# A span's state in one 128x256 tile and 64x64 products, and a new order for the last quarter of w_out and six loads

## The chip, the cores and the metric

The kernel runs on one core of a Trainium2 chip. The time is the device time of one execution in microseconds; the figure compared is the median of several executions. A profile of one execution shows each engine's instructions. The engines are TensorE (PE; its weight loads PEld), VectorE (DVE), ScalarE (ACT), GpSimd (POOL) and SyncE (SP, which only issues transfers here). Each works through its own queue in order and waits on semaphores. Matrix products leave their results in PSUM[...]; VectorE and ScalarE carry them from there to SBUF.

## The reference

Blocked linear attention with a decay per head, and a gated two-layer network on its result. There are 4 batches, 8 heads, 768 positions and 64 numbers per head; blocks of 64 positions; the network goes from 512 to 2048 and back, over 3072 tokens.

```python
for b in range(nb):
    intra = np.einsum('bhic,bhjc->bhij', qb, kb) * Dmask[None]
    intra = np.einsum('bhij,bhjd->bhid', intra, vb)
    inter = np.einsum('bhid,bhde->bhie', qb * lam_pow[None], kv_state)
    out[:, :, sl] = intra + inter
    kv_state = lam_block * kv_state + np.einsum('bhsd,bhse->bhde', kb_dec, vb)
x = out.transpose(0, 2, 1, 3).reshape(B * S, H * D)
h = x @ w_in
return (h * np.cos(h)) @ w_out
```

## The kernel before

**Tiling.** Tokens are worked in 24 sets of 128 ("blocks" in the code). The first four belong to two *spans*: span x is the first 256 positions of batch x, two positions to a partition. The rest form *ordinary pairs* 2 to 11 of two sets each, the same 128 positions of two batches. The network takes its tokens in nine tiles (`TILES`), the first of 512, most of 256. For each tile there are 16 hidden tiles f0 to f15 (L732: four products each, then a cosine on ScalarE, L738, and a product on VectorE, L744), and for each 128 tokens j four groups of four output products (L778), one group for each quarter of w_out. The first tile's hidden tiles f0 to f4 are made in two halves of 256 tokens, span 0's (columns 0 to 255) and span 1's.

**Stages.** At the start q and k of the spans are loaded (SP), scaled (L593; span 1's k on GpSimd), transposed on TensorE (L601) and copied (L604). Scores (L612), masks (L617) and values (L638) follow in two halves, *hp* 0 and 1, of four heads. The state that the second 128 positions of a span take from its first 128 is made by L625 from rows 0 to 63 (two heads at a time, 64x128 products of which only the diagonal 64x64 blocks are wanted), cast block by block into the block-diagonal `kv_bd` (L629, two instructions), and read by four full 128x128 products (L644), which add to the values in PSUM. `kv_bd` is filled with zeros beforehand (L217). Casts L652 then write `xT`, the input of the hidden products. Later, L697 makes the state at the end of both spans for pair 2.

An ordinary pair has six loads, q_f, k_f and v_f twice; scaled or cast copies (L329, L333, L337); transposes (pair 2 on TensorE, L359, later ones by DMA from SP's queue, L365); scores L407, mask L412, values L470 (L487 is a one-element copy that makes two row halves take turns), state products L419, sums L425, casts L430, carried products L502.

**What sets the order.** A planner at build time. Each piece of work is a task with an engine, an assumed length, what it depends on and a priority; the planner sets them on a time line, and each engine's queue has the order of that line. So changed assumed lengths move instructions. Between TensorE's tasks, until a certain hidden tile, `keep_awake` puts filler products into gaps of the plan (L866, 128x512 in bf16; L870 in f32). Loads of the spans, of w_in and w_out and of the pairs are issued in the order of the string `ORDER`: q, k, v with a number are loads from SP (spans' v from GpSimd), i0 to i5 pieces of w_in and o0 to o3 quarters of w_out, from GpSimd. In it o3 waited for the landing of the first load of pair 2 (q4, its first q_f), and v4 for k4; q4 itself waits, before and after, for tile 0's f13 (`pace`).

## Time and profile before

| | us |
|---|---|
| median of three executions | 202.84 (202.67 to 203.12) |
| the profiled execution | 202.54 |
| its span, first to last instruction | 200.80 |
| mean granted TensorE clock | 0.998 |

```profile
PE   6999999999999999999999999999999999999994
DVE  3978771269756948758458575835588354444001
ACT  4878771149658768666639666644887564345120
POOL 5893003085235360635555353545500000000000
DMA  5999999999889997999999899979910010111112
```

Each digit is the busy share of a fortieth of the span (5.02 us) in tenths; 9 is 90% or more. TensorE is at 9 from the second slice to the last but one. The DMA engines are at 9 or near it until seven tenths of the span, when the loads are done.

In the chain of waits, a row is the start, the length, and the engine with the tile, the line and the number of instructions; rows follow each other in time. In the time line of one engine, the second column is the time from the first start to the last modelled end, so neighbouring rows can overlap; the difference between two starts is what the first group really took from the engine. "DMA to landing" tells the least, the median and the most time from a transfer's issue to its end.

### The profile page before, as it was taken

To read this page: it belongs to the slowest core of one execution; us is meant where nothing else is said; L and a number is where in the kernel's file an instruction comes from. 1 tells how busy PE (TensorE), PEld (TensorE's weight loads), DVE (VectorE), ACT (ScalarE), POOL (GpSimd) and SP (SyncE) were. 2 spreads that over 40 slices of the span, in tenths; PEclk is the share of its full clock that TensorE was granted. 3 is DMA by queue.
4 is the path that set the end of the run, shared out by engine and by line. 5 is a ranking of instruction groups with operands and counts; after the bars stand their busy time and mean duration, and the time that the engine had idled before them with its cause. 6 is when DMAs were issued, how large, how long until landed. Compare 5 with 4: busy or idle time off the path is not lost.

```text
span 200.8 us, 5951 instructions
## 1 busy us (share of the span) xinstructions
PE 195.9 (98%) x2473; PEld 116.8 (58%) x2473; DVE 116.3 (58%) x230; ACT 119.4 (59%) x241; POOL 64.9 (32%) x85
## 2 busy tenths in 40 slices
PE   6999999999999999999999999999999999999994
PEld 3477444558757757766658676755445544444452
DVE  3978771269756948758458575835588354444001
ACT  4878771149658768666639666644887564345120
POOL 5893003085235360635555353545500000000000
PEclk9999999999999999999999999999999999999999
DMA  5999999999889997999999899979910010111112
GB/s 163 303 190 204 203 199 216 209 238 225 200 197 225 262 202 177 239 179 253 189 275 245 188 207 194 277 141 261 243 23 3 3 52 0 52 55 52 52 52 104
DMA packets 96620, 33.93 MB, mean 169 GB/s; under 512 B 84690, under 2 KB 93650, under 8 KB 96594
## 3 DMA queue, kind: packets, MB, share of 16 engines
q1 hardware_dynamic: 89088, 28.78, 63.2%
q0 software_dynamic: 7360, 4.72, 16.4%
q8 instruction: 19, 0.31, 0.7%
q10 hardware_dynamic: 146, 0.07, 0.1%
q14 instruction: 7, 0.06, 0.1%
HBM read 27.26 MB, written 6.29 MB: 167 GB/s over the span
## 4 chain that ended last, share of the span: by engine, by line
PE 95%; DMA 2%; ACT 0%; DVE 0%; SPq 0%; issue 0%; ACTq 0%; DVEq 0%
PE ps_h L732 42%; PE ps_f L778 42%; DMA sp_f<-in_k_dram 2%; PE ps_s L407 2%; PE ps_o L502 2%; PE ps_o L470 2%; PE ps_kv L419 1%; PE ps_t L601 1%; PE ps_s L612 1%; PE ps_o L638 1%; PE ps_kv L625 1%; PE ps_x L470 0%; PE ps_idle L870 0%; PE ps_t L359 0%; DVE k_sp L593 0%; PE ps_o L644 0%
## 5 line engine op out<-in xcount | busy, mean ns | idle before, releaser
L744 DVE TENSOR_TENSOR g<-ps_h,cos 128x256 bf16<-128x256 f32 (+1 forms) x149 | 73.1, 501 | 42.0 <-ACT cos L738 41.1
L738 ACT ACTIVATE cos<-ps_h,halfpi 128x256 f32<-128x256 f32 (+1 forms) x149 | 75.9, 536 | 29.3 <-PE ps_h L732 28.2
L778 PE MATMUL ps_f<-w_out_sb,g 128*128 128x512 bf16 (+2 forms) x400 | 91.4, 371 | 0.0
L732 PE MATMUL ps_h<-xT,w_in_sb 128*128 128x256 bf16 (+1 forms) x596 | 91.1, 303 | 0.0
L732 PEld LDWEIGHTS <-w_in_sb 128*128 128x128 bf16 x596 | 57.5, 98 | 30.1 <-DVE xT L510 0.4
L778 PEld LDWEIGHTS <-g 128*128 128x128 bf16 x400 | 37.6, 98 | 37.2
L329 POOL TENSOR_TENSOR qk<-q_f,q_scale 128x512 bf16<-128x512 f32 x19 | 20.0, 1067 | 34.7 <-DMA q_f<-in_q_dram 17.6
L792 ACT COPY o_sb<-ps_f 128x512 f32<-128x512 f32 (+1 forms) x24 | 13.7, 572 | 24.7 <-PE ps_f L778 24.5
L337 POOL TENSOR_TENSOR v_s<-v_f,v_scale 128x512 bf16<-128x512 f32 x19 | 19.6, 1042 | 9.8 <-DMA v_f<-in_v_dram 5.2
L412 DVE TENSOR_TENSOR s_m<-ps_s,mask 128x512 bf16<-128x512 f32 x20 | 13.0, 685 | 4.2 <-PE ps_s L407 3.6
L333 POOL CAST qk<-k_f 128x512 bf16<-128x512 f32 x18 | 11.0, 611 | 10.4 <-DMA k_f<-in_k_dram 10.2
L510 ACT CAST xT<-ps_o 128x512 bf16<-128x512 f32 x11 | 6.0, 588 | 9.0 <-PE ps_o L502 5.6
L425 DVE TENSOR_TENSOR sum<-sum,ps_kv 128x512 f32<-128x512 f32 x15 | 10.2, 682 | 0.6
L430 ACT CAST S<-sum 128x512 bf16<-128x512 f32 x15 | 9.1, 616 | 0.9 <-DVE sum L425 0.8
L253 POOL DMA_DIRECT2D w_out_sb<-in_moe_w_out_dram x4 | 3.0, 784 | 15.8 <-DMA q_f<-in_q_dram 15.8
L792 DVE COPY o_sb<-ps_f 128x384 f32<-128x384 f32 x1 | 0.6, 557 | 11.6 <-DMA out_dram<-o_sb 11.6
L470 PEld LDWEIGHTS <-v_s 64*64 64x64 bf16 x320 | 4.0, 107 | 4.2 <-issue 3.4
L870 PE MATMUL ps_idle<-blank 128*128 128x512 f32 (+2 forms) x8 | 4.7, 707 | 1.7 <-DVE blank L215 1.7
L487 DVE COPY spare<-ps_o 1x1 f32<-1x1 f32 x6 | 0.9, 156 | 8.4 <-PE ps_o L470 8.4
L617 DVE TENSOR_TENSOR s_m_sp<-ps_s,mask_sp 128x512 bf16<-128x512 f32 x8 | 5.1, 684 | 1.2 <-PE ps_s L612 1.2
L470 PE MATMUL ps_o<-s_m,v_s 64*64 64x64 bf16 x256 | 5.2, 196 | 0.0
L502 PE MATMUL ps_o<-qkT,S 64*64 64x64 bf16 x304 | 4.9, 195 | 0.0
(76 smaller groups left out, 90.1 us busy)
## 6 DMA issues: line engine op xcount, KB each, us to landing
q_f<-in_q_dram SPq DMA_DIRECT2D x20, 256.0 KB, 3.9
k_f<-in_k_dram SPq DMA_DIRECT2D x20, 256.0 KB, 4.2
v_f<-in_v_dram SPq DMA_DIRECT2D x20, 256.0 KB, 5.1
out_dram<-o_sb SPq DMA_DIRECT2D x19, 256.0 KB, 2.5
w_out_sb<-in_moe_w_out_dram POOLq DMA_DIRECT2D x4, 512.0 KB, 12.4
sp_f<-in_q_dram SPq DMA_DIRECT2D x2, 512.0 KB, 4.9
sp_f<-in_k_dram SPq DMA_DIRECT2D x2, 512.0 KB, 5.5
w_in_sb<-in_moe_w_in_dram POOLq DMA_DIRECT2D x2, 512.0 KB, 8.9
```

Source lines behind the costliest of these rows:

```text
L329: vec[e].tensor_mul(new_qk()[:, 0, :, s], live.pop(("q_f", 2 * pr + s)), q_scale[:, c, :].unsqueeze(2).to_broadcast([P, H, D]))
L333: (nc.scalar.copy if early else nc.gpsimd.tensor_copy)(new_qk()[:, 1, :, s], live.pop(("k_f", 2 * pr + s)))
L337: vec[e].tensor_mul(live["v_s", 2 * pr + s], live.pop(("v_f", 2 * pr + s)), v_scale[:, c, :].unsqueeze(2).to_broadcast([P, H, D]))
L412: nc.vector.tensor_mul(t, live["s", pr][s], mask.unsqueeze(1).to_broadcast([P, H, D]))
L425: nc.vector.tensor_add(new, live["sum", pr, 0] if half else live["sum", pr - 1, 1], live["kv", pr][half])
L430: nc.scalar.copy(new_S(pr, half), live["sum", pr, half])
L470: yield lambda h=h: nc.tensor.matmul(o[halves[h % 2], h // 2], lhsT=live["v_s", n0 + s][m, h, :], rhs=live["s_m", n0 + s][m, h, :], start= ...
L732: nc.tensor.matmul(t[:, :n], lhsT=w_in_sb[:, kd, f * P:(f + 1) * P], rhs=live["xT", i][:, kd, at], start=(kd == 0), stop=(kd == KD - 1))
L738: nc.scalar.activation(c[:, :n], live["h", i, f, at.start][:, :n], AF.Sin, bias=halfpi)
L744: return nc.vector.tensor_mul(live["g", i][:, f, at], live.pop(("h", i, f, at.start))[:, :n], live.pop(("c", i, f, at.start))[:, :n])
L778: nc.tensor.matmul(live["f", i, j, piece][:, :width], lhsT=live["g", i][:, f, j * P:(j + 1) * P], rhs=w_out_sb[:, f, part], start=(f == 0) ...
L792: (nc.scalar.copy if eng == "ACT" else nc.vector.tensor_copy)(o[:, :width], live["f", i, j, piece][:, :width])
```

## The change

State of a span: one 128x256 tile `kv_sp`, heads 2p on partitions 0 to 63 and heads 2p+1 on 64 to 127, made by sixteen 64x64 products, cast by one ScalarE instruction, and read by eight 64x64 products behind a drain of TensorE. The zero fill goes.

```diff
-    kv_bd = consts.tile([P, 2, NP, P], BF16)
-    nc.vector.memset(kv_bd, 0.0)
+    kv_sp = consts.tile([P, SPANS, NP, D], BF16)
...
-            L["kv"] = bank(t.bank[0], [P, NP, P], F32, "ps_kv")
+            L["kv"] = bank(t.bank[0], [P, NP, D], F32, "ps_kv")
...
-                    nc.tensor.matmul(L["kv"][:, p, :], lhsT=L["k"][rows, s, 2 * p:2 * p + 2, :], rhs=L["v"][rows, s, 2 * p:2 * p + 2, :],
+                    for i, h in enumerate(halves):
+                        nc.tensor.matmul(L["kv"][h, p, :], lhsT=L["k"][rows, s, 2 * p + i, :], rhs=L["v"][rows, s, 2 * p + i, :],
...
-        def update_out(_, h, e):
-            (nc.scalar.copy if e == "ACT" else nc.vector.tensor_copy)(kv_bd[h, x, :, h], L["kv"][h, :, h])
+        def update_out(_, e):
+            (nc.scalar.copy if e == "ACT" else nc.vector.tensor_copy)(kv_sp[:, x], L["kv"])
...
         def carried(_):
+            nc.tensor.drain()
             for p in range(NP):
-                nc.tensor.matmul(L["o"][1][:, p, :].rearrange("e (s u) -> e s u", s=2),
-                                 lhsT=kv_bd[:, x, p, :], rhs=L["qT"][:, :, p, chunks[1][0]],
-                                 start=False, stop=True, skip_group_check=True)
+                for h in halves:
+                    nc.tensor.matmul(L["o"][1][h, p, :].rearrange("e (s u) -> e s u", s=2),
+                                     lhsT=kv_sp[h, x, p, :], rhs=L["qT"][h, :, p, chunks[1][0]],
+                                     start=False, stop=True, skip_group_check=True)
```

Loads: o3 is issued directly behind o2 and waits for no load; the six loads of pair 2 follow each other on SP, v4 without a wait for k4.

```diff
-ORDER = "q0 k0 q1 k1 v0 v1 i0 i1 i2 i3 i4 i5 o0 o1 o2 q4 q5 k4 k5 o3"
+ORDER = "q0 k0 q1 k1 v0 v1 i0 i1 i2 i3 i4 i5 o0 o1 o2 o3 q4 q5 k4 k5"
...
-        if name == f"v{2 * SPANS}":
-            deps = [load_t["k_f", 2 * SPANS]]
-        if name == "o3":
-            deps = [load_t["q_f", 2 * SPANS]]
```

Planner: other assumed lengths and starts, other priorities for pair 2, the spans' last state made free of pair 2's scores, and one more dependence, of pair 3's scores on the last VectorE product of the second network tile.

```diff
-    SETUP = {"POOL": 3.7, "DVE": 4.4, "ACT": 6.0, "SP": 0.85, "DMA": 1.95}
+    SETUP = {"POOL": 3.7, "DVE": 4.2, "ACT": 6.1, "SP": 0.85, "DMA": 1.95}
...
-        issue_t[name, n], load_t[name, n] = dma("SP", LOAD_US, 0.85, emit, prio, deps, get=name,
-                                                lat=1.9 if name == "v_f" and n < 2 * SPANS + 2 else 1.0)
+        issue_t[name, n], load_t[name, n] = dma("SP", 0.95 if n < 2 * SPANS + 2 else LOAD_US, 0.85, emit, prio, deps, get=name,
+                                                lat=1.0)
...
-                t = pl.add("PE", MM(P, 8), src + ([T[pr, 0]] if i else []), partial(transposes, i=i), pa(-0.05 + 0.05 * i), banks=1)
+                t = pl.add("PE", MM(P, 8), src, partial(transposes, i=i), pa(-0.05 + 0.05 * i) if pr > SPANS else -900.0, banks=1)
...
-        us = {"DVE": 0.69, "POOL": 1.04}
+        us = {"DVE": 0.62, "POOL": 1.02}
...
-            s1 = pl.add("PE", 0.42, outs, partial(scores, hp=hp), pa(0.1 + 0.1 * hp), banks=2)
+            s1 = pl.add("PE", 0.33, outs, partial(scores, hp=hp), pa(0.1 + 0.1 * hp), banks=2)
...
-        u = pl.add("PE", 16 * QUART + SW, span_deps + s_t.deps, update, prio, banks=1)
-        u.then = s_t
-        s_t.deps.append(u)
+        u = pl.add("PE", 16 * QUART + SW, span_deps + [load_t["q_f", 2 * SPANS]], update, -900.0, banks=1)
...
+                if f == KF - 1:
+                    gates[i] = d
...
-    first_scores, first_update = add_scores(SPANS, prio_attn(2 * SPANS, 0.2))
+    first_scores, first_update = add_scores(SPANS, -900.0)
...
+        if i and pr in alone and pr in (3,):
+            alone[pr].deps.append(gates[i])
```

In the program that results, these queues differ from before. TensorE: a filler of 128x512 stands before the first hidden product; two hidden tiles, f0 and f1, not three, stand before span 1's second values; L697 stands alone between output products, two groups ahead of the transposes of pair 2, which stand some 2 us later in the queue than before; the scores of most later pairs stand a few hidden or output groups earlier. VectorE: pair 2's v_s stands before its two masks. ScalarE: the cast of the spans' last state stands before pair 2's two k casts. SP: the DMA transposes of pairs 3 and 4 stand before a store that they followed.

More of the change, by code (lines that the diff above doesn't have):

```diff
@@ L34 @@
 VALUES_OUT = [("ACT", "ACT"), ("DVE", "ACT")]
-STATE_OUT = [("ACT", "ACT"), ("ACT", "ACT")]
-ORDER = "q0 k0 q1 k1 v0 v1 i0 i1 i2 i3 i4 i5 o0 o1 o2 q4 q5 k4 k5 o3"
+STATE_OUT = ["ACT", "ACT"]
+ORDER = "q0 k0 q1 k1 v0 v1 i0 i1 i2 i3 i4 i5 o0 o1 o2 o3 q4 q5 k4 k5"
 W_IN = [2, 2, 1, 3, 4, 4]
@@ L624, in update @@
                 for s in range(2):
-                    nc.tensor.matmul(L["kv"][:, p, :], lhsT=L["k"][rows, s, 2 * p:2 * p + 2, :], rhs=L["v"][rows, s, 2 * p:2 * p + 2, :],
-                                     start=(p == 0 and s == 0), stop=True, skip_group_check=True)
-        def update_out(_, h, e):
-            (nc.scalar.copy if e == "ACT" else nc.vector.tensor_copy)(kv_bd[h, x, :, h], L["kv"][h, :, h])
+                    for i, h in enumerate(halves):
+                        nc.tensor.matmul(L["kv"][h, p, :], lhsT=L["k"][rows, s, 2 * p + i, :], rhs=L["v"][rows, s, 2 * p + i, :],
+                                         start=(p == 0 and s == 0), stop=True, skip_group_check=True)
+        def update_out(_, e):
+            (nc.scalar.copy if e == "ACT" else nc.vector.tensor_copy)(kv_sp[:, x], L["kv"])
         def values(task, hp):
@@ L668, in add_span @@
                 t.bank_frees = [[outs[-1]]]
-            s1 = pl.add("PE", 0.42, outs, partial(scores, hp=hp), pa(0.1 + 0.1 * hp), banks=2)
+            s1 = pl.add("PE", 0.33, outs, partial(scores, hp=hp), pa(0.1 + 0.1 * hp), banks=2)
             if x and hp == 0:
                 s_first = s1
-            so[hp] = [pl.add("DVE", 0.69, [s1], partial(scores_out, hp=hp, i=i), pa(0.1 + 0.1 * hp + 0.05 * i)) for i in range(2)]
+            so[hp] = [pl.add("DVE", 0.61, [s1], partial(scores_out, hp=hp, i=i), pa(0.1 + 0.1 * hp + 0.05 * i)) for i in range(2)]
             s1.bank_frees = [[t] for t in so[hp]]
-        u = pl.add("PE", 0.42, v_t + kt + [spans[0].get("carried")], update, pv(0.1), banks=1)
-        Uo_sp[x] = [pl.add(e, 0.4 if e == "ACT" else 0.42, [u], partial(update_out, h=h, e=e), pv(0.1))
-                    for h, e in zip(halves, STATE_OUT[x])]
+        u = pl.add("PE", 0.28, v_t + kt + [spans[0].get("carried")], update, pv(0.1), banks=1)
+        Uo_sp[x] = [pl.add(STATE_OUT[x], 0.4, [u], partial(update_out, e=STATE_OUT[x]), pv(0.1))]
         u.bank_frees = [Uo_sp[x]]
         span_deps.extend(v_t + kt)
-        v0 = pl.add("PE", 0.35, so[0] + v_t + [spans[0].get("carried")], partial(values, hp=0), pv(0.2), banks=2)
-        v1 = pl.add("PE", 0.35, [v0] + so[1], partial(values, hp=1), pv(0.25))
-        second = pl.add("PE", MM(P, 4) + 0.1, [v1] + Uo_sp[x], carried, pv(0.3))
+        v0 = pl.add("PE", 0.33, so[0] + v_t + [spans[0].get("carried")], partial(values, hp=0), pv(0.2), banks=2)
+        v1 = pl.add("PE", 0.33, [v0] + so[1], partial(values, hp=1), pv(0.25))
+        second = pl.add("PE", 0.25, [v1] + Uo_sp[x], carried, pv(0.3))
         for c, (t, e) in enumerate(zip((v1, second), VALUES_OUT[x])):
@@ L711, in add_span_state @@
         u.bank_frees = [[x]]
-    h_last, o_last = {}, {}
+    h_last, o_last, gates = {}, {}, {}
     hid, closing = [], None
@@ L838 @@
         prepare(pr)
-    first_scores, first_update = add_scores(SPANS, prio_attn(2 * SPANS, 0.2))
+    first_scores, first_update = add_scores(SPANS, -900.0)
     add_span_state(first_scores, prio_attn(2 * SPANS, 0.2))
     pr = SPANS
+    alone = {}
     for i in range(len(TILES)):
@@ L844 @@
             if pr + 1 in ALONE:
-                add_scores(pr + 1, prio_attn(2 * pr + 2, 0.2))
+                alone[pr + 1] = add_scores(pr + 1, prio_attn(2 * pr + 2, 0.2))[0]
             add_stretch(pr, first_update if pr == SPANS else None)
```

## The prediction

> **What bounds the kernel now.** I read the page first: busy shares, then the chain that ended last, then the chain in order of time, then TensorE alone from 10 to 17 us.

> ```profile
> PE 195.9 (98%) x2473; PEld 116.8 (58%) x2473; DVE 116.3 (58%) x230; ACT 119.4 (59%) x241; POOL 64.9 (32%) x85
> PE 95%; DMA 2%; ACT 0%; DVE 0%; SPq 0%; issue 0%; ACTq 0%; DVEq 0%
> ```

> TensorE is busy for 98% of the span and carries 95% of the chain. A busy PE need not be a full one, so the chain in order of time has to show whether anything but matmuls stands in it.

> ```profile
> 10.57 0.40 PE ps_t L601 x4
> ...
> 16.31 12.68 PE ps_h L732 x72
> 28.99 6.04 PE ps_f L778 x28
> ...
> 39.38 0.62 PE ps_kv L697 x32
> 40.00 0.38 PE ps_s L407 x32
> ```

> From 10.57 us to the end each piece starts where the one before it stopped. The large pieces run at one rate: 6.04/28 = 0.216 us for an output product (512 columns); in a later row 6.55/60 = 0.109 us for a hidden product of 256 columns. By these rates the 72 products of the second line (28 of 256 columns, 44 of 512) need 3.06 + 9.49 = 12.55 us, so only 0.13 us of waiting is in them (the load of weights at 16.69 waited for a w_in piece). So from 16 us on nothing can be won by earlier data; only fewer TensorE instructions, fewer changes of shape, or that 0.13 us count, and any new wait costs its full length. What may be won otherwise lies before 16 us:

> ```profile
> 10.90 0.62 PE L625 MATMUL ps_kv<-v_sp,k_sp 64*128 64x128 bf16 x8
> 11.45 0.42 PE L638 MATMUL ps_o<-s_m_sp,v_sp 64*64 64x128 bf16 x16
> 11.69 0.39 PE L612 MATMUL ps_s<-qT_sp,kT_sp 64*64 64x128 bf16 x16
> ...
> 12.70 0.40 PE L644 MATMUL ps_o<-qT_sp,kv_bd 128*128 128x128 bf16 x4
> 13.03 0.62 PE L625 MATMUL ps_kv<-v_sp,k_sp 64*128 64x128 bf16 x8
> ...
> 14.14 1.48 PE L732 MATMUL ps_h<-xT,w_in_sb 128*128 128x256 bf16 x12
> 15.56 0.42 PE L638 MATMUL ps_o<-s_m_sp,v_sp 64*64 64x128 bf16 x16
> 15.91 0.40 PE L644 MATMUL ps_o<-qT_sp,kv_bd 128*128 128x128 bf16 x4
> ```

> The first column is the start; the difference to the next start is what a group costs. Here ScalarE is near:

> ```profile
> 12.93 1.08 ACT L652 CAST xT<-ps_o 128x512 bf16<-128x512 f32 x2
> ```

> The first hidden product (14.14) needs both casts, which end at 14.01.

> [...] the 16 products of L638 cost 0.24 us where the next group is 64*64 too (11.45 to 11.69) and 0.35 where it is not (15.56 to 15.91), both behind a change: 0.10 us for one change. The forecast counts them at that price. [...]

> ```profile
> DMA to landing us min/median/max: 13.3/14.3/15.2
> DMA to landing us min/median/max: 6.6/6.6/6.6
> DMA to landing us min/median/max: 3.3/3.5/3.8
> DMA to landing us min/median/max: 6.2/6.4/6.7
> ```

> In order: quarters 1 and 2 of w_out (issued 15.19 and 15.92, landing 28.5 and 31.1, so 2.6 us apart); quarter 3 (32.55, 39.1); the two q_f of pair 2 (28.74 and 29.15; 32.0 and 32.9); its two v_f (33.89 and 34.31; 40.1 and 41.0). Both times the first load landed 0.9 us behind a quarter under way, and the next 0.9 us later. I go by the trace: loads land behind the quarter, 0.9 us apart.

> **The change part by part.**

> *The zero fill of kv_bd* (0.48 us of VectorE at 1.66) goes; VectorE then idles until 3.93 anyway: nothing.

> *State products.* L625 costs 0.55 us: 0.45 of work and a change. The new form has 16 products 64*64 of 64 columns, of which two run side by side (both use rows 0 to 63). Nearest row: L697, also in twos, (0.62 - 0.10)/32 = 0.016 us each, so 0.26. Span 0 saves 0.19 and the change to L638 behind it, 0.29 in all; span 1 saves 0.19 and both its changes, 0.39. The single cast frees 0.37 us of ScalarE (L629: two take 0.74) at 11.55, where it idles 0.16 us before the next copy anyway: nothing.

> *Carried products.* Eight 64*64 of 128 columns, two by two, cost what four full ones do (12.70 to 13.03 less a change): 0.23. The change before them goes, but a drain stands there. The trace has no drain. From below 0.10[...]; from above 0.6: the tail of a group, 0.18 (it ends 0.42 after its start but costs 0.24), and 0.4, the longest stretch that the list of waits puts down to "issue" before a weight load. I take 0.25, tail and one weight load. Span 0: -0.10 + 0.25, and its change to L625 is counted above. Span 1: the change in front goes, one behind it (to L732) comes: +0.25.

> *What of this is on the path.* Up to the first hidden product the sum is -0.29 - 0.39 - 0.10 + 0.25 = -0.53, but it can't show. k_sp on GpSimd, the transposes, the kT copy (to 11.59), the scores, the second transposes and copy (12.45 to 13.03) and the xT casts keep their times, as each waits for the one before, not for L625. And the order of the changed program has a new filler product (128x512, 0.21 us, with a change) before the first hidden one. So that starts at 14.06 to 14.15 where it was 14.14: I take -0.05.

> *From there to f5* (the first 512-column hidden tile) the set of products is the same; only two hidden tiles instead of three stand before span 1's second values. Those need VectorE's last mask product, which with scores 0.25 us earlier ends near 15.05 and is awaited for some 0.05. Drain: +0.25. The wait for w_in (0.13) vanishes, as f4, whose piece lands at 16.65, now comes after 17.5. Sum -0.05 + 0.05 + 0.25 - 0.13 = +0.12.

> *State of the spans* (L697) moves ahead by itself, between output products; before, it adjoined the scores L407. One more change: +0.10. Counting changes through both orders from 16 us to the end gives 34 and 35, all other products equal in number.

> *w_out's quarter 3 and the six loads.* The quarter is issued by GpSimd at about 16.7, not at 32.55, and needs no wait for q_f any more; nothing but qk of pair 2 stands behind it there. It lands at 31.1 + 2.6 = 33.7. The loads, still held by L744's f13 until 28.74 on SP, then land at 34.6, 35.5 (q), 36.4, 37.3 (k), 38.2, 39.1 (v) instead of 32.0 to 41.0: q later, v earlier. TensorE asks for them in a new order: transposes of q at 37.4 (VectorE and GpSimd ready 36.6), of k at 38.7 (ScalarE first casts the span state until 37.3, then k twice until 38.4), scores at 41.0, values at 43.2. For these VectorE runs v_s ahead of the masks (two, 1.29): 41.5 to 42.85. All covers hold, the smallest by 0.3 us. No wait was there before, so nothing is won: 0. If the cover fails, the excess is paid in full.

> *SP's and the later order.* Transposes of pairs 3 and 4 go ahead of a store, and scores of pairs 4 to 11 move up against the hidden products by up to 2 us. qkT landed 0.7 us or more ahead of the new places even at the old times, and the stores have no reader: 0. The gate on pair 3's scores waits for a VectorE product done 0.7 us earlier: 0.

> **Sum.** +0.12 + 0.10 = +0.22 us. The profiled execution took 202.54 (span 200.80, 1.74 around it), giving 202.76; the median of the runs shown is 202.84, 0.3 above the profiled one. On that base 203.06, rounded to 203.05.

> **Rivals.**
> *Slower, by pair 2's loads.* Before quarter 3 the old run has an empty gap: k's last load landed near 34.7, the quarter at 39.1 took 2.6, so 1.8 us moved nothing, with v's loads already issued. If such a gap now stands between quarters 2 and 3, all six loads slide by it. GpSimd's qk is then ready at 36.6 + 1.8 = 38.4 where TensorE's queue holds the transposes L359 at 37.4, with every output product behind them: 1.0 us, and 204.1 in all. It decides from a gap of 0.8. For: the old gap. Against: the quarter is now queued behind another[...].
> *Faster: TensorE's saving counts in full.* The chain names TensorE before 14 us too. If the casts come earlier with it and a drain costs 0.10: -0.68 up to the first hidden product, then 0.10 - 0.13 + 0.10, in all -0.61; 202.2. Against: the chain of copies and casts, and the filler.
> *Not what it says:* moved scores or a transposed load find their data late somewhere after 46 us (stalls of a few tenths, pair 4 or 6): 203.6. For: places moved by 1 to 2 us; against: the margins above.

> **Chances.** My forecast 0.67, with its own range 202.75 to 203.55 (drain 0.1 to 0.6, and some 0.15 for the median); loads 0.17; faster 0.07; later stalls 0.09. What a measurement here can tell from no change is 0.2%, 0.4 us. Of my forecast 0.53 lies within it and 0.14 above; so faster 0.07, same 0.53, slower 0.40. Range 202.6 to 203.9: it leaves out the faster case and most of the loads' one.

> **What would show it.** Right: first L732 at 14.1; the carried products start about 0.3 us behind the values' last issue, not 0.15; f5 some 0.1 later than its old 18.45; L697 between L778 rows with 0.1 us on both sides; quarter 3 landing near 33.7 and v near 39; output products after 46 us offset by a constant 0.2. Wrong: f5 earlier than 18.3 (path not ScalarE's), idle TensorE before L470 near 43, or an offset that grows later.

## The result, and the profile after

| | before | changed |
|---|---|---|
| median of 4 runs (range), us | 202.86 (202.67 to 203.12) | 204.80 (204.56 to 204.88) |
| ratio, 95% interval | | 1.0088, 1.0064 to 1.0113 |
| profiled execution, its span | 202.54, 200.8 | 204.72, 203.0 |

The change costs 1.94 us; 0.2 was forecast, 203.9 was the upper end. The page of the changed kernel, engines and chain:

```profile
PE 194.8 (96%) x2475; PEld 118.2 (58%) x2502; DVE 115.5 (57%) x229; ACT 118.5 (58%) x239; POOL 64.8 (32%) x85
PE 93%; issue 2%; DVE 2%; ACT 2%; ACTq 0%; DVEq 0%
```

The span is 2.2 us longer. The 194.8 us against 195.9 don't mean less work: 27 products lack in the records (2,475, with 2,502 weight loads, one for each product; before 2,473 and 2,473), and the changed kernel with the old fillers (e9 below), whose records are complete, has 196.5. "issue" went from 0% of the chain to 2%: time in which the engine waited for nothing that the profile shows. The chain in order of time says where (start, length, what):

```profile
13.80 1.08 ACT xT L654 x2
14.93 1.03 PE ps_h L731 x8
15.96 0.29 PE ps_o L638 x12
16.25 0.54 issue
16.79 0.25 PE ps_o L638 x4
17.16 0.41 PE ps_o L646 x8
...
37.57 0.62 PE ps_kv L698 x32
38.20 0.16 issue
...
131.07 0.48 ACT cos L737
131.55 0.52 ACT S L429
132.06 0.60 PE ps_h L731 x4
```

Three things stand out. The first hidden product comes at 14.93, not 14.14. Sixteen products of one line, span 1's values, are torn into 12 and 4: the last of the 12 issued at 16.04, the next at 16.79, with no semaphore between. And at 132 us another engine stands in the chain where only TensorE stood before (eight hidden products in a row from 131.32). The 0.16 of "issue" at 38.20 is none: the weight load of the next product is there at 38.14, the product itself is one of those that lack. Weight loads tell a true gap. Since a profile is one execution, two of each kernel are set side by side (the second ones are e10 and e4 below):

| us | before | before, again | changed | changed, again |
|---|---|---|---|---|
| first hidden product | 14.14 | 14.70 | 14.93 | 14.40 |
| first output product | 28.82 | 29.28 | 30.50 | 30.22 |
| between the two | 14.68 | 14.58 | 15.57 | 15.82 |
| fifth o_sb copy | 57.34 | 57.80 | 59.12 | 58.92 |
| span | 200.8 | 201.3 | 203.0 | 202.9 |

The means of the two differ by 0.24 us at the first hidden product, 1.31 at the first output product, 1.45 at 57 us and 1.9 at the end. So the 1.9 us are 0.24 of front, 1.07 between 14 and 30 us, 0.14 in the stretch with the span state, and 0.45 late, at 132 us. The front is scatter as much as change: the two executions of one kernel differ by 0.5 us there. One part of it is no scatter. From the last transposes of span 1 (12.02 and 12.57 us before, 12.52 and 11.99 in the change) to the first hidden product it is 2.12 and 2.13 us before, and 2.41 both times in the change. ScalarE's row of the change tells why:

```profile
13.80 1.07 ACT L654 CAST xT<-ps_o 128x512 bf16<-128x512 f32 x2 [0.27 <-PE ps_o L646]
```

In the new program the two casts of span 0 have changed places, which the list of changed queues above leaves out: the first one now waits for the last carried product, behind the drain, and the second has no wait of its own. Before, the first began at 12.93, before the last carried product had ended.

The transfers did what was forecast, up to k. The landing rows of quarters 0 and 1, 2 and 3 of w_out (issued at 14.5, 15.2, 15.9 and 16.7), then of the two q_f of pair 2 (30.4 and 30.8):

```profile
DMA to landing us min/median/max: 11.7/12.6/13.5
DMA to landing us min/median/max: 13.5/15.3/17.1
DMA to landing us min/median/max: 4.3/4.5/4.8
```

Quarter 3 landed at 33.8 (33.7 forecast), q at 34.7 and 35.6 (34.6 and 35.5), the first k at 38.1 (36.4), v at 39.7 and 40.6 (38.2 and 39.1); TensorE waited for none of them.

### The profile page after: what moved, and what is told of

Its sections match the earlier page's. It is cut to its first block, busy times and chain, and to the rows that moved or that the text cites. A ratio compares the mean times of both kernels' runs of the same rounds, so it can differ in the third digit from the quotient of the medians.

```text
span 203.0 us, 5981 instructions
## 1 busy us (share of the span) xinstructions
PE 194.8 (96%) x2475; PEld 118.2 (58%) x2502; DVE 115.5 (57%) x229; ACT 118.5 (58%) x239; POOL 64.8 (32%) x85
## 4 chain that ended last, share of the span: by engine, by line
PE 93%; issue 2%; DVE 2%; ACT 2%; ACTq 0%; DVEq 0%
PE ps_h L731 41%; PE ps_f L779 40%; PE ps_idle L870 3%; PE ps_s L406 1%; PE ps_o L501 1%; PE ps_o L469 1%; PE ps_kv L418 1%; PE ps_t L600 1%; DVE sum L424 1%; DVE s_m L411 1%; PE ps_s L611 1%; ACT xT L654 1%; PE ps_x L469 0%; ACT cos L737 0%; PE ps_t L358 0%
## 5 line engine op out<-in xcount | busy, mean ns | idle before, releaser
L737 ACT ACTIVATE cos<-ps_h,halfpi 128x256 f32<-128x256 f32 (+1 forms) x149 | 75.8, 537 | 30.7 <-PE ps_h L731 30.4
L779 PE MATMUL ps_f<-w_out_sb,g 128*128 128x512 bf16 (+2 forms) x377 | 88.4, 370 | 2.2 <-issue 1.4
L336 POOL TENSOR_TENSOR v_s<-v_f,v_scale 128x512 bf16<-128x512 f32 x19 | 19.7, 1044 | 16.8 <-DMA v_f<-in_v_dram 14.5
L870 PE MATMUL ps_idle<-blank 128*128 128x512 f32 (+3 forms) x12 | 5.9, 620 | 1.7 <-DVE blank L215 1.7
L520 DVE TENSOR_TENSOR xT<-ps_o,cross 128x256 bf16<-128x256 f32 x8 | 3.1, 422 | 3.8 <-PE ps_o L501 3.8
## 6 DMA issues: line engine op xcount, KB each, us to landing
w_out_sb<-in_moe_w_out_dram POOLq DMA_DIRECT2D x4, 512.0 KB, 14.4
```

What stands on the lines that cost most here:

```text
L336: vec[e].tensor_mul(live["v_s", 2 * pr + s], live.pop(("v_f", 2 * pr + s)), v_scale[:, c, :].unsqueeze(2).to_broadcast([P, H, D]))
L737: nc.scalar.activation(c[:, :n], live["h", i, f, at.start][:, :n], AF.Sin, bias=halfpi)
L779: nc.tensor.matmul(live["f", i, j, piece][:, :width], lhsT=live["g", i][:, f, j * P:(j + 1) * P], rhs=w_out_sb[:, f, part], start=(f == 0) ...
L870: nc.tensor.matmul(idle_ps[:, :n], lhsT=blank[:, :P], rhs=blank[:, :n], start=True, stop=True)
```

## The experiments

Two theories were set up. **S, instruction supply**: TensorE's instructions arrive in blocks, and the change, with 24 products more (48 instructions, as each has a weight load) and two drains, reaches the end of a block before the next is there. **F, late front**: new filler products, and a TensorE clock that rises late (7.75 us in the profile of the change, 5.4 before), hold up everything ahead of the first hidden product. What led to S is the page's row of the queue that carries instructions:

```profile
q8 instruction: 19, 0.31, 0.6%
```

Its columns are packets, MB and share of the time. That is 16.4 KB a packet (16,384 bytes in the trace), and 19 packets for TensorE's some 5,000 instructions, so about 256 each (of all kernels here, those with up to 5,030 have 19 packets, those with 5,086 and more have 20). In the trace the first one starts at 14.38 us; the view of the transfers from 14.1 to 14.4 us has it:

```profile
q8 instruction: 1, 0.02, 19.8%
```

**e1 and e2: each half of the change alone.**

```
e1: before, with kv_sp, its 64*64 products, one cast, the drain
e2: changed, with kv_bd, its 128x128 products, two casts, the zero fill
```

> The kernel before with the state part alone: one 128x256 tile, 64x64 products, one cast, the drain; order of loads, lengths in the planner and fillers as before. Instruction supply (theory S: TensorE's stream comes in blocks; the instructions after about the 450th are there only from 16.75 us on, and the changed kernel gets to that point 1.7 us sooner because its state products are twice as many): TensorE gets there at about 15.7 us, in the second half of span 1's values, and stands still until 16.75, 1.0 us for nothing that the profile names; with 0.2 for the drains the time is 204.0. Late front (theory F: fillers and the TensorE clock): the fillers are the old ones, so the first hidden product comes at 14.1 as before, nothing stalls at 16 us, and the time is 203.1. Drain alone (as predicted): 203.1.

> The changed kernel with the old state tile and its 128x128 products (and the zero-fill), everything else as in the change. S: the 450th instruction is a hidden product at about 18 us, so there is no stall at 16 us; what is left is the late front, 0.7 to 0.8, and the extra change of shape, 0.1: 203.7. F: the late front makes nearly all of the 2 us, so 204.5. If the first hidden product comes at 14.1 here, the late front belongs to the state part.

e1 took 205.29 us (203.87 to 206.59; ratio 1.0103, 1.0061 to 1.0146), e2 203.29 (1.0014, 1.0004 to 1.0025). The state part alone has the stall, again inside span 1's values (15.98 to 16.68, 0.70 us from the last issue before it to the first after; all stalls below are given so); the rest alone has none. F falls as the main cause: e2's first hidden product came later (15.10) than that of e1 (14.39) or of the change, and e2 is the faster one by 2 us. The rest alone costs 0.4, which leaves 1.2 to 1.5 of the change to the state part. e1's second cost was not foreseen. Rows of SyncE, GpSimd, ScalarE and TensorE in its profile, which is the slowest of its six executions (206.59):

```profile
31.15 2.08 SPq L252 DMA_DIRECT2D k_f<-in_k_dram  x2
33.17 0.74 POOL L252 DMA_DIRECT2D w_out_sb<-in_moe_w_out_dram  x1 [16.46 <-DMA q_f<-in_q_dram]
39.69 0.62 ACT L332 CAST qk<-k_f 128x512 bf16<-128x512 f32 x1 [3.58 <-DMA k_f<-in_k_dram]
40.36 0.62 PE L358 MATMUL ps_t<-ident,qk 128*128 128x128 bf16 x8 [2.06 <-ACT qk L332]
```

With the old order of loads, quarter 3 went out while the second k_f was under way, and this k_f was used at 39.69 instead of 35.61 as before: 2.06 us of idle TensorE. So e1's time says little on the state part by itself. In the new order quarter 3 lands at 33.8, ahead of all six loads; how often the race is lost with the old order is not shown.

**e3, e4: more instructions in the kernel before; the change again.**

```
-  matmul(idle_ps, lhsT=ident, rhs=ident.unsqueeze(1).to_broadcast([P, 4, P]))
+  for j in range(8):
+      matmul(idle_ps[:, 64 * j:64 * j + 64], lhsT=ident, rhs=ident[:, :64])
```

> The kernel before, with each of its three 512-column fillers on ident issued as eight of 64 columns: the same columns, 42 more instructions ahead of the first hidden product, the computation untouched. S: the 450th instruction is now in the second half of span 1's values at 15.7 us, and TensorE stands still there until about 16.75: +1.0, 203.9. F and the drain: no change, 202.9.

> The changed kernel once more, for the scatter of its profile. S: the same stall at the same instruction, 16.1 to 16.8 us. If the stall is an accident of one execution, it is not there, and the time is the same all the same. F: if the late TensorE clock (full only from 7.75 us in the first profile, 5.4 before) belongs to the kernel, it is at 7.75 again; if it is chance, it lies elsewhere, and the first hidden product moves with it while the time stays within 204.6 to 204.9 only if something later sets it.

e4: 204.51 (1.0072, 1.0047 to 1.0097). The stall is at the same instruction, 15.51 to 16.51, 1.00 us where the first execution has 0.76, although the front was 0.5 us earlier: TensorE ran ahead and waited longer. The clock rose at 6.48. So the clock is chance and the stall is not. e3: 203.76 (1.0042, 1.0024 to 1.0061), the expected size by luck, since the place is another. The packet started at 13.41, in time; there was no stall at 16 us. Instead a piece of w_in landed at 15.88 (14.94 before), and TensorE stood 0.56 us waiting for it; and 0.57 us went at 132 us, by "issue", where the kernel before has 0.11 from load to load:

```profile
132.69 0.83 PE L732 MATMUL ps_h<-xT,w_in_sb 128*128 128x256 bf16 x6 [0.29 <-issue]
```

This stall and those of the changed kernel (131.56 to 132.06), e4 and e1 stand at one number in the records of TensorE, the 3,756th or 3,757th. The records lack 21 products by then. Counted by weight loads, which are complete, 3,777 instructions are out in each of the four, and the one that is held up is the 3,778th = 450 + 13 x 256. In each, TensorE goes on 2.3 to 2.4 us after the fourteenth packet starts (129.69 and 132.06 in the changed kernel). The ACT that the profile names for it in the changed kernel is a coincidence: in e4 that cast ended 0.15 us before TensorE went on.

**Where the end of a block falls.** The rows below give, for the stretch from 0 to within the stall, the length, then busy time and count of TensorE's products and of its weight loads; the kernels are the changed one, e11, e6 and e5 in turn:

```profile
0.00:16.50 16.50, 14.26 (x222) 9.33 (x223) 10.44 (x21) 10.65 (x22) 13.07 (x27) 1.00 1.19 216
0.00:16.60 16.60, 14.59 (x223) 9.67 (x224) 11.48 (x24) 11.78 (x25) 13.17 (x27) 1.00 1.18 216
0.00:15.50 15.50, 13.03 (x223) 9.36 (x223) 9.67 (x20) 9.85 (x20) 12.14 (x26) 1.00 1.17 218
0.00:14.50 14.50, 11.83 (x223) 9.27 (x223) 8.64 (x18) 9.41 (x19) 10.98 (x24) 1.00 1.13 219
```

445, 447, 446 and 446 products and loads, with four, two, three and three sequencer instructions on top: 449 in each, whatever line they belong to and whenever they come. All eight kernels with a stall in the front have it there. The four without were still short of it when the block was usable (before: 429 at 16.75). The same count can be made for every end, 450 + 256 k, in all fourteen profiles: 255 ends. The first instruction behind an end is never issued less than 2.27 us after the end's packet starts. It was 2.27 to 2.53 us in the 13 cases with a stall (nine in the front, four at 132 us), and 2.54 us or more in the 242 without.

**e11: the cleanest test of S.** The kernel before with the span state's products in halves:

```
-  matmul(kv[:, p, :], lhsT=k[rows, s, 2*p:2*p+2, :], rhs=v[rows, s, 2*p:2*p+2, :])
+  for i, h in enumerate(halves):
+      matmul(kv[:, p, h], lhsT=k[rows, s, 2*p:2*p+2, :], rhs=v[rows, s, 2*p+i, :])
```

> The kernel before with each 128x128 product of the span state issued as two of 64 columns: the same tile, values, casts and columns, no drain, no other order; 32 instructions more ahead of the first hidden product. S: the block's end moves 32 instructions forward, to the last carried products of span 1 at about 16.1 us, and TensorE stands still there until 16.7: 0.5 to 0.7, with up to 0.3 more at 132 us, where the end comes close to the last attention products; 203.5. If instructions cost only their columns: 202.9.

203.33 us (1.0019, 1.0005 to 1.0033). The same columns, and a stall of 0.48 us in the middle of four carried products, behind the 449th instruction:

```profile
16.19 0.29 PE L645 MATMUL ps_o<-qT_sp,kv_bd 128*128 128x128 bf16 x2
16.74 0.27 PE L645 MATMUL ps_o<-qT_sp,kv_bd 128*128 128x128 bf16 x2 [0.26 <-issue]
```

(The start of the third against that of the second is what counts; the 0.26 is what is left of it after the modelled end of a product.)

**e5, e6, e7: the end of the block moved on purpose,** by about 112, 56 and 112 instructions more in the fillers (e7 also with the old fillers):

```
e5, e6: ident fillers of 512 columns as 8 of 64 (as in e3; e5's last one as 4 of 128)
e5, e7: + float32 filler at 3.5 us as ident products of 64 columns
e7:     + no new fillers (those of the kernel before)
```

> The changed kernel with the same filler columns ahead of 9 us issued as 112 more instructions (the float32 filler at 3.5 us as 39 products of 64 columns, three of the ident fillers as eight each); nothing else. Theory S, sharpened by the first runs: TensorE's stream comes in blocks of 256 instructions (16 KB each on the instruction queue), [...] With 112 more in front, the ends fall at 13.4 us, where TensorE waits for xT anyway, and around 126.6 us, ahead of the burst of attention products: both stalls go, 0.75 to 1.0 and 0.5 us, and the time is 203.3. If the stalls belong to the products concerned and not to where the blocks end: 204.6 as the changed kernel.

> The changed kernel with its four ident fillers issued as eight products of 64 columns each, 42 more instructions ahead of the first hidden product and 56 in all; the same columns. S: the ends of the blocks now fall where the 256 instructions ahead of them are densest: about 1.3 us of stall right at the first hidden products (14.5 us) in place of 0.75 to 1.0, and about 3 us at 127 to 128 us in place of 0.5; 207.5, the worst of all. If instructions cost only their own time: 204.6.

> As e5_rows_112 with the fillers of the kernel before in place of the new ones (no float32 filler of 128 columns, no extra 64 columns, no ident filler ahead of the first hidden product, one ident filler ahead of the scores fewer), in as many instructions. If the new fillers delay TensorE while its clock is still low (the first hidden product came at 14.39 and 14.59 us with old fillers and a clock that rose at 7.9 and 8.4 us, at 14.93 and 15.10 with the new ones and 7.8 and 8.3): 0.3 to 0.5 less than e5_rows_112, 202.9. If the late front is the clock's chance alone: the same as e5_rows_112.

e5 204.21 (1.0069, 1.0048 to 1.0090), e6 204.61 (1.0098, 1.0070 to 1.0127), e7 204.21 (1.0067, 1.0049 to 1.0086). None came where it was expected (203.3, 207.5 and 202.9). Right: the stall moved to the same count, in e5 among the state products (13.47 to 14.92), in e6 into a filler (14.66 to 15.94; 1.3 expected, 1.28 measured),

```profile
14.66 0.20 PE L867 MATMUL ps_idle<-ident 128*128 128x64 bf16 x1
15.94 0.38 PE L867 MATMUL ps_idle<-ident 128*128 128x64 bf16 x7 [1.08 <-issue]
```

and the late stall was gone in e5. Wrong: that a block is usable 5.1 us after TensorE enters the one before, the author's estimate from the first profiles (16.79 less 11.64 in the changed kernel). In e5 and e7 TensorE entered it (the 193rd instruction, 449 less 256) at 8.6 and 8.2, yet the packet started only at 12.4 and 12.0, 3.8 us later (2.1 to 3.4 in the other kernels); so the front stall grew to 1.45 and 1.24 us. And e6 had no late stall at all: the packet started 1.7 us before TensorE issued the first instruction of the block before, in a stretch of slow products, and the 1.6 us in which TensorE ran through that block cost nothing. e7 took as long as e5, the branch of its expectation in which the late front is chance; but with a stall in both fronts, neither can show what the fillers cost. What holds in all eight stalled kernels is the second half: TensorE goes on 2.3 to 2.5 us after the packet starts. What the packet waits for in these 3.8 us, no trace shows.

**e8, e9, e10: what the fillers cost.** e8 is e2, e9 the changed kernel, both with the fillers of the kernel before; e10 is that kernel again.

> As e2_rest_only (the changed kernel with the old state tile and its 128x128 products), with the fillers of the kernel before as well: what is left of the change is the order of loads, the gate on pair 3, the moved waits and the planner's lengths. S with the fillers: no block ends inside a burst, so nothing stalls, the 0.4 of e2_rest_only were the new fillers, and the time is that of the kernel before, 202.9 (+0.1 for the extra change of shape at 37 us). If the 0.4 belong to the order of loads or the gate: 203.3 again.

> The changed kernel with the fillers of the kernel before, nothing padded. The first hidden product comes 0.3 to 0.5 sooner at the same clock. S: that gains nothing, since TensorE then waits for the block that is fetched at 14.2 us and usable at 16.6: 204.4 to 204.6. If the late front and the stall added up: 204.2 or less.

> The kernel before once more, for the scatter of its profile. The TensorE clock rose at 5.4 us in its first profile and at 6.4 to 8.4 in the others; if that is chance, it lies elsewhere here, and with a rise at about 8 us the first hidden product comes at 14.4 to 14.6 instead of 14.15. S: no stall at the 450th instruction, which it reaches about 17.8 us, a microsecond after the block is usable.

e8 203.48 (1.0030, 1.0012 to 1.0049), e9 204.13 (1.0057, 1.0036 to 1.0078), e10 202.86 (1.0007, 0.9987 to 1.0027). e10's clock rose at 6.93 and its first hidden product came at 14.70, with 0.44 us more span and no stall. e9 stalls 0.49 us (16.17 to 16.66) and not at 132 us, where ten instructions fewer put the block's end out of the way; it gains 0.4 on e4 and 0.7 on the first figure of the change. By its number that is the other branch of the expectation (204.2 or less, front and stall adding up), but the late stall that it lost is worth 0.45 by itself, so a gain from the front is not shown. e8's expectation failed: the 0.4 of the rest are not its fillers. In its profile TensorE waited twice (0.35 us net at 90, about 0.6 at 114) for a transposed copy, because the change asks for scores earlier there:

```profile
90.67 0.33 PEld L407 LDWEIGHTS <-qkT 64*64 64x64 bf16 x32 [0.78 <-DMA qkT<-qk]
114.31 0.45 PE L407 MATMUL ps_s<-qkT 64*64 64x64 bf16 x32 [0.45 <-DMA qkT<-qk]
```

e2 and the changed kernel show no such wait. At 90 us they are 0.5 and 1.3 us behind e8, and the copy is there. At 114 us e2 is only 0.16 behind, but its SP began that pair's transposes 2.7 us sooner (104.62, in e8 107.29). Of the 0.4 of the rest the swapped casts explain a part (2.23 us from the last transposes to the first hidden product in e8 and 2.36 in e2, 2.12 before); how much of the median comes from this, from such waits or from the fillers stays open.

**e12: work put ahead of the stall.**

```
+ spans[1]["carried"].deps.append(hid[4])   # f2 ahead of span 1's drain
```

> As e9_change_old_fillers with one more order in the plan: the third group of hidden products (f2, four products of 256 columns) ahead of span 1's drain and carried products. S: TensorE does f2's 0.44 us of work while it waits for the block of instructions that is usable at 16.6 to 16.7 us, and while it drains; what stands still there falls from 0.5 plus 0.3 to 0.2 to 0.4 together, and the time is 203.7, still above the kernel before. If f2 waits for something else there (its gate's bank or xT), the time is that of e9_change_old_fillers, 204.1.

204.22 us (1.0071, 1.0057 to 1.0085), no gain on e9. The four products of f2 were split: one at 15.67, three at 16.77. The expectation forgot that f2's instructions also lie beyond the end of the block: whatever comes after the 450th instruction waits until 16.7 us, in any order. No kernel here beats the one before.

## Why the prediction was wrong

**The step that failed is the sum in "From there to f5".** It counted products, changes, drains and waits for data, as if an instruction that waits for nothing is there to be issued. Its terms add up: 0.25 for the drain, 0.05 for the mask and -0.13 for the w_in piece make 0.17 between the first hidden product and the 512-column tiles, and the changed kernel needs 15.57 - 14.68 = 0.89 us more up to the first output product, of which 0.70 is the stall (0.76 less the 0.06 to the next product that would have passed anyway): 0.19 is left. In the second pair it is 15.82 - 14.58 = 1.24, less 0.95: 0.29. There the kernel before had no wait for w_in to lose (its 72 hidden products from 16.73 on take 12.55 us, the bare rate), so 0.30 was due. The stall was not among the terms, nor the rivals. The rival "slower" chose the loads of pair 2, whose covers held. The 1.8 us gap that it rests on was misread from landings: before quarter 3 the DMA engines are down to some 30 GB/s for 0.5 us only (34.5 to 35.0), and carry over 100 before and after.

**State and carried products.** Right in size: with both groups, span 0's carried and span 1's state products took 0.40 us (13.36 to 13.76) where they took 0.88 (12.70 to 13.58). But the step costed the new form by TensorE time alone. Twice as many state products, said to save 0.68 us that cannot show, are what costs: e11 has as many, without drain or reordering, and stalls 0.48.

**The drain** (0.25 taken, 0.1 to 0.6 bounded, the 0.1 being the author's estimate from the 0.10 of one change of shape): the carried products issue 0.31 us (span 0) and 0.36 (span 1) after the last values, near the 0.3 named as the sign.

**First hidden product at 14.1** (-0.05): measured 14.93 and 14.40, but 14.14 and 14.70 before. The step took one execution's start for the kernel's. It also said that the xT casts keep their times, and put a wait at nothing: with the casts in their new order both stand behind the carried products and the drain, and from the last transposes on 0.29 us is lost where -0.05 was taken. It takes both halves: the state alone (e1) needs 2.05 us there, the rest alone 2.23 (e8), the change 2.41, with the new fillers or the old (e9). Ahead of these transposes the new fillers may add 0.2 (12.42 on average in the three profiles with them uncut, 12.22 in the seven with the old ones uncut); with such scatter that is not shown. The stall behind it hides what the front loses: TensorE goes on 2.4 us after the packet starts, in the earlier execution (16.51) and in the later one (16.79).

**Alone in the row, the span state** (+0.10): from the first output product to the fifth copy the two pairs differ by 0.10 and 0.19; the change of shape was not measured by itself. **Loads and the gate** (0): right for the time, though k and v came 1.5 us later than worked out, as SP spent 2.3 us on issuing one k.

**SP's and the later order** (0): the 0.45 us at 132 us are another end of a block, the fourteenth, shown by e3, e1 and e4 at the same count, by the packet 2.3 to 2.4 us ahead, and by their absence in e5, e6, e7 and e9, where that end lies elsewhere or the packet came sooner. The fear of late transposed copies was right for the rest alone (e8), not for the whole.

So the 1.9 us by which the two pairs of profiles differ (1.94 in the medians) are about 0.8 of stall at the 450th instruction, 0.25 of drain and what goes with it behind the first hidden product, 0.15 in the stretch of the span state, 0.45 of stall at the 3,778th, and 0.25 of front.

## What to carry to other kernels

Count instructions as well as microseconds: splitting products into smaller ones that TensorE runs side by side saved its time here (0.40 us where it was 0.88) and still doubled what had to be fetched, and a stretch of 256 instructions that TensorE could run through in under some 5 us (4.6 to 6.3 us from the entry into a block to the use of the next, in the fronts that stalled) may stall (it need not: e6 ran through one in 1.6 us, with a slow stretch ahead of it). A tear in the middle of a group of like products, put down to "issue", found at the same instruction count in every execution and ended 2.3 to 2.5 us after a packet of the instruction queue starts, is the sign; test it with the same columns in more instructions. Compare a second execution before an offset of half a microsecond in the front is explained, and measure from a near event that both have: that brought out the swapped casts.

## What the runs showed of the hardware

The TensorE clock rose to full at 5.4, 6.4, 6.5, 6.9, 7.6, 7.7, 7.75, 7.9, 8.3, 8.35 and 8.4 us in eleven profiles with nearly the same work ahead of it (5.4 and 6.9 in the kernel before, 7.75 and 6.5 in the changed one). In the changed kernel's first profile a transposing product (L600) takes 0.107 us from issue to issue at 5.83 to 6.26, and 0.056 at 8.14 to 8.36. What sets the rise, no trace shows. In these two kernels the execution with the later rise has the later first hidden product, 14.70 against 14.14 and 14.93 against 14.40; but e3, with the columns of the kernel before, has it at 14.59 with a rise at 8.4. How much of an offset in the front is the clock's is not shown.
